# Two feed-forward layers on one core: one more weight pair converted in the first layer, and the second layer's weight requests and input splits at other places

## The chip, the cores and the metric

The program runs on one core of a Trainium2 chip. The time is device microseconds (us) of one execution; lower is better. Three executions of the kernel before are shown, and one more was recorded by the hardware profiler.

## What is computed

An attention with packed keys feeds two dense layers, in float32. Shapes: batch 4, 8 heads, 576 positions, head size 64, 32 packed positions; then x has 2304 rows of 512, and each layer goes 512 to 2048 to 512.

```python
def _attn_ref(q, k, v, p):
    p_packed = sm_attn(p, k, v)
    out = sm_attn(q, p_packed, p_packed)

def _moe_ref(x, w_in, w_out):
    h = x @ w_in
    g = np.maximum(h, 0.0) + np.log1p(np.exp(-np.abs(h)))
    return g @ w_out

def _moe2_ref(x, w_in, w_out):
    h = x @ w_in
    g = h * (1.0 / (1.0 + np.exp(-h)))
    return g @ w_out
```

The weights arrive as 64-bit floating-point numbers; the kernel reads them as pairs of 32-bit words and builds float32 values from them.

## The kernel before

All work is written out in the order in which each engine is to do it: the program's instructions are queued per engine in the order of the code, nothing reorders them, and each engine works its queue front to back. SyncE (SP) issues every transfer, also front to back: a transfer that has to wait for its buffer holds up all transfers behind it.

**Precision.** Every operand of a matrix product is split into a high part (ScalarE rounds it, a copy to the type float32r) and a low part (VectorE subtracts the high part). A product is then three matmuls: low by high, high by low, high by high.

**First layer** (0 to about 370 us). Attention comes first, then 128 short steps (`run_steps`). Each does one 128-wide slice of the hidden layer for 288 rows of x: six matmuls (L482), softplus and split (L494, L495, L499), and twelve matmuls of the output product (L522), added into `ya` (L539). Between them an `agenda` (a list of items by step) places other work: the first layer's own weight conversions (`conv_w`), and conversions for the second layer.

**Conversions for the second layer.** `wi2` comes in 16 slices, two of which make a *pair* `jp` (0 to 7); `wo2` in 16 slices `n`. A conversion of a pair (`conv_pair`, or the fills of `plan_second`) loads two raw slices (`load_raw`, L186), scales them (ScalarE, L135), joins the words (VectorE, L197 and L203), forms four differences (`sums_i`, L218), rounds (`high_i`, L221), subtracts (`low_i`, L225) and stores 1792 KB to a scratch area `wd` in HBM (`store_i`, L232). A slice of `wo2` goes the same way (`high_o` L242, `low_o` L246) and is stored as 512 KB into `od` (`store_o`, L250). In the kernel before, pairs 0 to 2 and slices 0 to 11 are done in the first layer; pairs 3 to 7 and slices 12 to 15 in steps 1 to 5 of the second layer.

**Second layer** (`second`, from about 370 us). 24 steps `k`: three blocks `s` of 768 rows by eight pairs. A step does a 2 by 2 block of the input product with seven products `Q1` to `Q7` in place of eight (a scheme of Strassen's kind, hence the sums and differences), six matmuls of 128 by 384 each (`products`, L833), and four output tiles of twelve matmuls each (`out_tile`, L849), which belong to results of earlier steps. Tile `y0` to `y3` of step k is of group f = (k-2)//2 and needs the split results `G` of steps 2f and 2f+1. Step 1 has no output tiles, step 0 carries the first layer's last ones. In the PE queue of a usual step stand: Q1, Q6, y0, Q2, Q7, y1, Q5, y2, Q3, Q4, y3. ScalarE reads bank A after Q1 (`ta`, L887), and after Q2 applies the silu (`tg`, L901) and splits into `G`; VectorE adds (`add`, L883) `u2`, `u3` and `c2`; Q3 has to wait for the sum `c2` that reads bank C. After Q3 and Q4 come silu and split of `tc` (L926) and `c2` (L938, L939).

**Rings.** The converted weights come back from HBM in chunks of 512 KB: `w<-wd` (`load_i1`, L775; one chunk holds two products' weights) into a ring of five buffers, a chunk requested when the chunk five before it has been used; `w<-od` (`load_o1`, L780) into a ring of eight buffers, two chunks at the end of each step. A chunk of `wd` whose pair isn't stored yet is held back (`held`) until the store is issued; it then waits for the store to land. Group f uses chunks 4f to 4f+3 of `od` in steps 2f+2 and 2f+3.

**Points.** A step calls `go(...)` at fixed places, at which the fills of that point are emitted: L at the start, A0 and D0 after Q6, D1 and A1 ahead of y1, D2 after Q5, S ahead of the last silu, A3 and D3 at the end. The raw and split buffers of the second layer's conversions (the pool `stage`, opened at the end of step 0) lie where the first layer's buffers lay; from step 6 on `xc1`, the split input of block 1, takes their place. `x_sum`, `x_high`, `x_low` (L560, L563, L567) make the split input of the next block, in steps 6 to 8 and 14 to 16.

Of the kernel before, what the change touches and what calls it, by code (L numbers as in the profile page):

```python
# [9 lines left out]
F32R = mybir.dt.float32r  # L10
# [7 lines left out]
P = 128  # L18
B, H, S, D = 4, 8, 576, 64
# [4 lines left out]
NF = DFF // P  # L24
# [3 lines left out]
D1 = D + 1  # L28
# [4 lines left out]
GJ = 4  # L33
# [5 lines left out]
NSUP = T // (2 * N1)  # L39
NJ = NF // 2  # L40
NW = 2 * P
NQ = 7
RI = 5
Q1, Q6, Q2, Q7, Q5, Q3, Q4 = range(NQ)
# [3 lines left out]
def body(ctx, tc, kT, vv, qT, pT, wi1, wo1, wi2, wo2, out):  # L48
# [57 lines left out]
    def plan_load(fn, step):  # L106
        loads.setdefault(step, []).append(fn)
# [3 lines left out]
    wraw, whl, wo_plain = {}, {}, {}  # L111
# [60 lines left out]
    st, raws, o_hl = {}, {}, {}  # L172

    def open_stage(wx_bufs, **kw):
        st["p"] = p = push(stage_stack, "stage", 1, **kw)
        st["wf"] = p.tile([P, NQ + 1, NW], F32, name="wf")
        st["whl"] = p.tile([P, NQ, 2, NW], F32R, name="whl2")
        st["wx"] = wx_bufs

    def close_stage():  # L180
# [37 lines left out]
            nc.vector.tensor_tensor(out=wf[:, o], in0=wf[:, a], in1=wf[:, b], op=ALU.subtract)  # L218

    def high_i(a, b):  # L220
        nc.scalar.activation(out=st["whl"][:, a:b, 0], in_=st["wf"][:, a + 1:b + 1], func=AF.Copy)  # L221

    def low_i(a, b):
# [323 lines left out]
    def xq(s, t, k):  # L547
# [5 lines left out]
    SUMS = {  # L553
        Q5: (X22, X21, X22, ALU.add), Q7: (X21, X11, X21, ALU.subtract),
        Q6: (X11, X22, X11, ALU.subtract), Q3: (X12, X12, X11, ALU.subtract),
    }
# [38 lines left out]
    def plan_all():  # L595
# [15 lines left out]
            plan_load(lambda k=k, n=n: load_w(k, n), load)  # L611
            plan(Item(conv_w(k, n)), (s, s + 1))

        for jp, ss in enumerate(((4, 5, 8, 9, 12), (36, 37, 40, 41, 44), (65, 66, 67, 68, 69))):
            ss = tuple(base(1) + s for s in ss)
            for n in 2 * jp, 2 * jp + 1:
                plan_load(lambda n=n: load_raw("i", n, 3), ss[0] - 4)
            plan(Item(conv_pair(jp)), ss)
            plan_load(lambda jp=jp: store_i(jp), ss[-1])
        for n, s in enumerate((15, 18, 21, 28, 47, 50, 53, 60, 71, 72, 73, 75)):  # L620
            s += base(1)
            plan_load(lambda n=n: load_raw("o", n, 3), s - 3)
            plan(Item(conv_o(n)), (s, s + 1))
            plan_load(lambda n=n: store_o(n), s + 1)
        s = base(3) + XC0
# [139 lines left out]
    fills = {}  # L765
# [11 lines left out]
    def load_o1(m):  # L777
        w = ring_o[m] = wp.tile([P, 2 * DM], F32R, name="w", tag=f"o{m % RING['o']}")
        c = m % NF * 2 * DM
        nc.sync.dma_start(out=w.bitcast(F32), in_=od[:, c:c + 2 * DM])  # L780

    def fill(k, point, fn, *args):
        fills.setdefault((k, point), []).append(lambda: fn(*args))

    def plan_second():
        for jp in range(3, NJ):
            k = jp - 2
            for n in 2 * jp, 2 * jp + 1:
                fill(k - (jp > 3), "L" if jp > 3 else "L0", load_raw, "i", n, 0)
                fill(k, "A0", scale_raw, "i", n, True)  # L790
                fill(k, "D0", plain_i, n, True)
            fill(k, "D1", sums_i)
            fill(k, "A1", high_i, 0, 4)
            fill(k, "A1", high_i, 4, NQ)
            fill(k, "D2", low_i, 0, 4)
            fill(k, "D2", low_i, 4, NQ)
            fill(k, "S", store_i, jp)
        for n in range(12, NF):
            k = n - 11
            fill(k, "L", load_raw, "o", n, 0)  # L800
            fill(k, "A1", scale_raw, "o", n, True)
            fill(k, "D3", plain_o, n, True)
            fill(k + 1, "A0", high_o, n, 1)
            fill(k + 1, "D2", low_o, n)
            fill(k + 1, "S", store_o, n)
        for s in range(1, NSUP):
            for i, q in enumerate((Q1, Q2, Q4, Q5, Q7, Q6, Q3)):
                h, d = divmod(4 * (NJ * s - 2) + i, 4)
                if q in SUMS:
                    fill(h, f"D{d}", x_sum, s, q)  # L810
                fill(h, f"D{d}", x_high, s, q)
                fill(h + (d + 1) // 4, f"D{(d + 1) % 4}", x_low, s, q)

    def second():
        psa_stack.close()
# [50 lines left out]
        def out_of(k, i):  # L866
            if not k:
                (dm, y), = emit_out(NS + i)
                return lambda: finish_out(NS + i, dm, y)
            f, t = divmod(k - 2, 2)  # L870
            if f < 0:
                return lambda: None
            y = out_tile(f, t, i)
            return lambda: add_out(f, t, i, y)

        def step(k):
            nonlocal G
            go = lambda p: [fn() for fn in fills.get((k, p), ())]
# [29 lines left out]
                y.pop(0)()  # L908
            go("D1")
            go("A1")  # L910
            y1 = out_of(k, 1)
            y1()
            products(k, Q5, b["C"], True)
# [28 lines left out]
            go("D3")  # L942
            for i, g in (0, g1), (1, g2):
                frees.setdefault(k // 2 * 2 + 2 + i, []).append(g)
            m = k // 2 * GJ + GJ + k % 2 * 2
            if m + 2 <= NSUP * NF and k > 0 or k == 0:
                for i in range(2):
                    if m + i < NSUP * NF:
                        load_o1(m + i)
            if k == 0:  # L950
                l0_stack.close()
                open_stage(1, side="right", reuse_waits="tile")
            if (k + 1, "L0") in fills:
                for fn in fills[k + 1, "L0"]:
                    fn()

        plan_second()
        for k in range(NSTEP):
# [63 lines left out]
```

## Time and profile before

| | |
|---|---|
| median of 3 runs | 809.77 us (808.24 to 809.95) |
| profiled execution | 810.95 us, of it the span of the profile 809.0 us |
| TensorE busy with matmuls | 764.9 us, 95% of the span |
| VectorE, ScalarE busy | 491.7 us (61%), 363.6 us (45%) |
| mean granted TensorE clock | 0.977 of 2.4 GHz |
| transfers | 145.90 MB, mean 180 GB/s |

The profile shows one execution on the engines PE (TensorE), PEld (its weight loads), DVE (VectorE), ACT (ScalarE) and SP (SyncE, which issues the transfers). Times run from the span's start. A row of the timeline merges equal instructions that follow each other; in brackets stands how long the engine was idle before the row and what released it. Busy shares alone say little here, since the second layer has stretches of different limits; the table by stretch below is cut at the first matmul of each step; its columns are the stretch and its length, the busy time of PE, PEld, DVE, ACT and POOL (instructions in brackets), the granted TensorE clock as a share of 2.4 GHz, the busy share of the transfer engines, and GB/s.

### The profile page before, as it was taken

To read this page: it belongs to the slowest core of one execution; us is meant where nothing else is said; L and a number is where in the kernel's file an instruction comes from. 1 tells how busy PE (TensorE), PEld (TensorE's weight loads), DVE (VectorE), ACT (ScalarE), POOL (GpSimd) and SP (SyncE) were. 2 spreads that over 40 slices of the span, in tenths; PEclk is the share of its full clock that TensorE was granted. 3 is DMA by queue.
4 is the path that set the end of the run, shared out by engine and by line. 5 is a ranking of instruction groups with operands and counts; after the bars stand their busy time and mean duration, and the time that the engine had idled before them with its cause. 6 is when DMAs were issued, how large, how long until landed. Compare 5 with 4: busy or idle time off the path is not lost.

```text
span 809.0 us, 13431 instructions
## 1 busy us (share of the span) xinstructions
PE 764.9 (95%) x5488; PEld 726.6 (90%) x5488; DVE 491.7 (61%) x915; ACT 363.6 (45%) x684; POOL 0.7 (0%) x6
## 2 busy tenths in 40 slices
PE   8999999999999999999598787999999999999998
PEld 7777899999999999999598786999999999999998
DVE  4898877888589878574555663743234564334342
ACT  3687776565456555453342442432323332342230
POOL 0000000000000000000000000000000000000000
PEclk9999999999999999999789699999999999999999
DMA  9944231433543416062885949183562644825602
GB/s 341 344 152 171 84 152 54 163 111 106 183 154 121 156 65 237 27 234 79 286 334 208 375 175 328 75 325 122 204 259 61 252 171 155 318 87 207 239 21 79
DMA packets 38972, 145.90 MB, mean 180 GB/s; under 512 B 4352, under 2 KB 7936, under 8 KB 37376
## 3 DMA queue, kind: packets, MB, share of 16 engines
q1 hardware_dynamic: 38912, 145.06, 48.6%
q8 instruction: 43, 0.70, 0.4%
q14 instruction: 17, 0.14, 0.1%
HBM read 117.25 MB, written 27.79 MB: 179 GB/s over the span
## 4 chain that ended last, share of the span: by engine, by line
PE 75%; DMA 13%; ACT 5%; DVE 4%; SPq 1%; issue 1%; ACTq 0%; DVEq 0%
PE y L522 23%; PE y L849 19%; PE h L482 12%; PE pC L833 6%; DMA w<-wd 6%; PE pA L833 4%; PE pB L833 4%; DMA od<-ohl 3%; PE pD L833 3%; PE psa L448 2%; DMA raw<-wo 2%; PE y L515 2%; DMA wraw<-wo 1%; DMA raw<-wi 1%; PE psa L355 1%
## 5 line engine op out<-in xcount | busy, mean ns | idle before, releaser
L849 PE MATMUL y<-G,w 128*128 128x384 f32 x1152 | 219.5, 340 | 7.0 <-ACT G L927 7.0
L849 PEld LDWEIGHTS y<-G,w 128*128 128x128 f32 x1152 | 206.5, 192 | 7.6 <-ACT G L927 7.3
L522 PE MATMUL y<-gh,w 128*128 128x288 f32 x960 | 213.0, 298 | 0.2 <-DVE ya L537 0.2
L522 PEld LDWEIGHTS y<-gh,w 128*128 128x128 f32 x960 | 160.2, 188 | 13.1 <-issue 4.6
L522 PE MATMUL y<-gl,w 128*128 128x288 f32 x480 | 142.0, 296 | 0.0
L482 PE MATMUL h<-ax,vw 128*128 128x288 f32 x768 | 125.3, 298 | 0.3 <-DVE ax L431 0.3
L482 PEld LDWEIGHTS h<-ax,vw 128*128 128x128 f32 x768 | 109.5, 188 | 2.5 <-DVE ax L431 0.5
L522 PEld LDWEIGHTS y<-gl,w 128*128 128x128 f32 x480 | 90.6, 189 | 0.5 <-DVE gl L499 0.5
L494 ACT ACTIVATE gt<-h 128x288 f32<-128x288 f32 x120 | 48.8, 406 | 86.6 <-PE h L482 81.9
L862 DVE TENSOR_TENSOR ya<-y,ya 128x384 f32<-128x384 f32 x72 | 40.0, 556 | 65.6 <-PE y L849 65.3
L499 DVE TENSOR_TENSOR gl<-gt,gh 128x288 fp32r<-128x288 f32 x120 | 54.3, 453 | 38.7 <-ACT gh L495 38.1
L833 PE MATMUL pA<-xc,w 128*128 128x384 f32 x288 | 61.1, 348 | 14.4 <-DMA w<-wd 11.0
L833 PE MATMUL pC<-xc,w 128*128 128x384 f32 x288 | 59.7, 342 | 12.5 <-DVE c L883 12.5
L833 PEld LDWEIGHTS pA<-xc,w 128*128 128x128 f32 x288 | 51.6, 194 | 18.6 <-issue 13.6
L833 PEld LDWEIGHTS pC<-xc,w 128*128 128x128 f32 x288 | 51.3, 191 | 13.7 <-DVE c L883 13.4
L833 PE MATMUL pB<-xc,w 128*128 128x384 f32 x288 | 61.2, 349 | 1.6 <-DVE tu L883 1.6
L883 DVE TENSOR_TENSOR tu<-ta,pB 128x384 f32<-128x384 f32 x48 | 26.5, 551 | 58.1 <-PE pB L833 55.5
L833 PEld LDWEIGHTS pB<-xc,w 128*128 128x128 f32 x288 | 53.2, 196 | 2.6 <-DVE tu L883 2.6
L495 ACT ACTIVATE gh<-gt 128x288 fp32r<-128x288 f32 x120 | 53.5, 445 | 3.8
L539 DVE TENSOR_TENSOR ya<-y,ya 128x288 f32<-128x288 f32 x104 | 46.9, 453 | 10.7 <-PE y L522 10.5
L926 ACT ACTIVATE tc<-tc 128x384 f32<-128x384 f32 x24 | 12.6, 523 | 90.5 <-DVE tc L883 90.3
L901 ACT ACTIVATE tg<-pA 128x384 f32<-128x384 f32 x24 | 11.6, 485 | 63.3 <-PE pA L833 63.3
(90 smaller groups left out, 791.9 us busy)
## 6 DMA issues: line engine op xcount, KB each, us to landing
w<-wd SPq DMA_DIRECT2D x84, 512.0 KB, 6.8
w<-od SPq DMA_DIRECT2D x48, 512.0 KB, 6.1
wd<-whl SPq DMA_DIRECT2D x8, 1792.0 KB, 9.1
wraw<-wi SPq DMA_DIRECT2D x16, 512.0 KB, 5.8
wraw<-wo SPq DMA_DIRECT2D x16, 512.0 KB, 5.8
raw<-wi SPq DMA_DIRECT2D x16, 512.0 KB, 6.9
raw<-wo SPq DMA_DIRECT2D x16, 512.0 KB, 7.9
od<-ohl SPq DMA_DIRECT2D x16, 512.0 KB, 3.3
```

Source lines behind the costliest of these rows:

```text
L448: nc.tensor.matmul(t[32 * k:32 * k + 32, r, :512 if wide else 256], lhsT=pts[b][rows, k * NP:(k + 1) * NP], rhs=w[rows, :], start=True, st ...
L482: nc.tensor.matmul(h, lhsT=w, rhs=x, start=(i == 0), stop=(i == len(mm) - 1))
L494: nc.scalar.activation(out=gt, in_=h, func=AF.Softplus)
L495: nc.scalar.activation(out=gh, in_=gt, func=AF.Copy)
L499: nc.vector.tensor_tensor(out=gl, in0=gt, in1=gh.bitcast(F32), op=ALU.subtract)
L515: nc.tensor.matmul(y, lhsT=wo_plain[j][:, c], rhs=gs[u - 1, x], start=(j == js[0]), stop=(j == js[-1]))
L522: nc.tensor.matmul(y, lhsT=w[:, c], rhs=g, start=(j == js[0] and m == 0), stop=(j == js[-1] and m == 2))
L539: nc.vector.tensor_tensor(out=acc, in0=y, in1=acc, op=ALU.add)
L833: nc.tensor.matmul(out, lhsT=a, rhs=b, start=start and not i, stop=not start and i == len(mm) - 1, skip_group_check=True,)
L849: nc.tensor.matmul(y, lhsT=a[:, c], rhs=G[:, g, h, j], start=(k % 2 == j == m == 0), stop=(k % 2 == j == 1 and m == 2),)
L862: nc.vector.tensor_tensor(out=acc, in0=y, in1=acc, op=ALU.add)
L883: add = lambda o, i, j, op=ALU.add: nc.vector.tensor_tensor(out=o, in0=i, in1=j, op=op)
```

## The change

It moves one pair (jp = 3) and one slice of `wo2` (n = 12) from the second layer's conversions into the first layer, at new places in its agenda. In the second layer the raw slices of a pair are requested one step ahead at a new point M (between A1 and y1 of that step), the pool `stage` takes its buffer `whl` when `high_i` writes it and not when the pool opens, and `load_o1` asks for chunks of `od` one step later than before: at the end of step k for the chunks 2k+2 and 2k+3 (before: 2k+4 and 2k+5). The splits of x for the next block are spread by a table. No arithmetic is changed.

```diff
@@ -174,7 +174,6 @@
     def open_stage(wx_bufs, **kw):
         st["p"] = p = push(stage_stack, "stage", 1, **kw)
         st["wf"] = p.tile([P, NQ + 1, NW], F32, name="wf")
-        st["whl"] = p.tile([P, NQ, 2, NW], F32R, name="whl2")
         st["wx"] = wx_bufs
@@ -218,6 +217,8 @@
     def high_i(a, b):
+        if not a:
+            st["whl"] = st["p"].tile([P, NQ, 2, NW], F32R, name="whl2")
         nc.scalar.activation(out=st["whl"][:, a:b, 0], in_=st["wf"][:, a + 1:b + 1], func=AF.Copy)
@@ -611,13 +612,15 @@
-        for jp, ss in enumerate(((4, 5, 8, 9, 12), (36, 37, 40, 41, 44), (65, 66, 67, 68, 69))):
+        for jp, ss in enumerate(
+            ((4, 5, 8, 9, 12), (36, 37, 40, 41, 44), (65, 66, 67, 68, 69), (71, 72, 73, 74, 75))
+        ):
...
-        for n, s in enumerate((15, 18, 21, 28, 47, 50, 53, 60, 71, 72, 73, 75)):
+        for n, s in enumerate((15, 18, 21, 28, 47, 50, 53, 60, 24, 33, 56, 76, 77)):
             s += base(1)
@@ -783,10 +786,10 @@
     def plan_second():
-        for jp in range(3, NJ):
+        for jp in range(4, NJ):
             k = jp - 2
             for n in 2 * jp, 2 * jp + 1:
-                fill(k - (jp > 3), "L" if jp > 3 else "L0", load_raw, "i", n, 0)
+                fill(k - 1, "M", load_raw, "i", n, 0)
                 fill(k, "A0", scale_raw, "i", n, True)
...
-        for n in range(12, NF):
+        for n in range(13, NF):
             k = n - 11
...
         for s in range(1, NSUP):
-            for i, q in enumerate((Q1, Q2, Q4, Q5, Q7, Q6, Q3)):
-                h, d = divmod(4 * (NJ * s - 2) + i, 4)
-                if q in SUMS:
-                    fill(h, f"D{d}", x_sum, s, q)
-                fill(h, f"D{d}", x_high, s, q)
-                fill(h + (d + 1) // 4, f"D{(d + 1) % 4}", x_low, s, q)
+            plans = {
+                (0, "D0"): ((x_high, Q1), (x_high, Q2)),
+                (0, "D1"): ((x_high, Q4), (x_low, Q1)),
+                (0, "D2"): ((x_low, Q2), (x_low, Q4)),
+                (0, "D3"): ((x_sum, Q5),),
+                (1, "D0"): ((x_high, Q5), (x_sum, Q7)),
+                (1, "D1"): ((x_low, Q5), (x_sum, Q6), (x_high, Q7), (x_high, Q6)),
+                (1, "D2"): ((x_low, Q7), (x_low, Q6)),
+                (1, "D3"): ((x_sum, Q3),),
+                (2, "D0"): ((x_high, Q3),),
+                (2, "D1"): ((x_low, Q3),),
+            }
...
@@ -908,6 +920,7 @@
             go("D1")
             go("A1")
+            go("M")
             y1 = out_of(k, 1)
@@ -942,17 +955,13 @@
-            m = k // 2 * GJ + GJ + k % 2 * 2
-            if m + 2 <= NSUP * NF and k > 0 or k == 0:
-                for i in range(2):
-                    if m + i < NSUP * NF:
-                        load_o1(m + i)
+            m = (k + 1) // 2 * GJ + (2 - k % 2 * 2)
+            for i in range(2):
+                if GJ <= m + i < NSUP * NF:
+                    load_o1(m + i)
             if k == 0:
                 l0_stack.close()
                 open_stage(1, side="right", reuse_waits="tile")
-            if (k + 1, "L0") in fills:
-                for fn in fills[k + 1, "L0"]:
-                    fn()
```

How the order on the engines moves, at two places. First SP's queue from step 0's end into step 4, in the kernel before (L780 asks for chunks of `od`, L775 for chunks of `wd`, L186 for raw slices, L232 and L250 store):

```order
L780 DMA w<-od 128x1024 x2
L186 DMA raw<-wi 128x512 x4
L186 DMA raw<-wo 128x512
L775 DMA w<-wd 128x1024 x2
L232 DMA wd<-whl_5028 128x3584
L775 DMA w<-wd 128x1024 x2
L780 DMA w<-od 128x1024 x2
L186 DMA raw<-wi 128x512 x2
L186 DMA raw<-wo 128x512
L775 DMA w<-wd 128x1024 x2
L232 DMA wd<-whl_5028 128x3584
L250 DMA od<-ohl 128x1024
```

The same stretch with the change, from the five chunks of `wd` of steps 0 and 1 on (L778 is `load_i1`, L783 `load_o1`, L185 `load_raw`, L233 and L251 the stores):

```order
L778 DMA w<-wd 128x1024 x5
L185 DMA raw<-wi 128x512 x2
L778 DMA w<-wd 128x1024 x2
L783 DMA w<-od 128x1024 x2
L185 DMA raw<-wo 128x512
L778 DMA w<-wd 128x1024 x2
L185 DMA raw<-wi 128x512 x2
L233 DMA wd<-whl_5216 128x3584
L778 DMA w<-wd 128x1024
L783 DMA w<-od 128x1024 x2
L185 DMA raw<-wo 128x512
L778 DMA w<-wd 128x1024 x2
```

The two chunks of `od` at the end of step 0 are gone, step 1 has neither a raw slice of `wo2` nor a store, and the first store of a pair comes one step later.

Second, ScalarE's queue in step 1 and the start of step 2, in the kernel before (from step 1's `ta` to step 2's `tg`):

```order
L887 ACTIVATE ta<-pA 128x384
L135 ACTIVATE raw<-raw 128x512 x2
L901 ACTIVATE tg_5040<-pA 128x384
L902 ACTIVATE G<-tg_5040 128x384
L221 ACTIVATE whl_5028<-wf 128x4x256
L221 ACTIVATE whl_5028<-wf 128x3x256
L135 ACTIVATE raw<-raw 128x512
L926 ACTIVATE tc_5041<-tc_5041 128x384
L927 ACTIVATE G<-tc_5041 128x384
L938 ACTIVATE c_5042<-c_5042 128x768
L939 ACTIVATE G<-c_5042 128x768
L887 ACTIVATE ta<-pA 128x384
```

and with the change:

```order
L899 ACTIVATE ta<-pA 128x384
L913 ACTIVATE tg_5068<-pA 128x384
L914 ACTIVATE G<-tg_5068 128x384
L939 ACTIVATE tc_5069<-tc_5069 128x384
L940 ACTIVATE G<-tc_5069 128x384
L951 ACTIVATE c_5070<-c_5070 128x768
L952 ACTIVATE G<-c_5070 128x768
L899 ACTIVATE ta<-pA 128x384
L135 ACTIVATE raw<-raw 128x512 x2
```

The three scalings of raw slices and the two roundings that stood between step 1's `ta` and its last silu have left step 1.

## Rows read from the trace of the kernel before

**Rows 1.** Busy time by stretch, cut at the starts of steps 1 to 11.
```profile
383.60:399.10 15.50, 8.47 (x44) 8.15 (x43) 8.72 (x16) 5.41 (x9) 0.00 (x0) 0.79 0.72 242
399.10:422.40 23.30, 20.73 (x91) 19.97 (x91) 13.14 (x24) 10.51 (x19) 0.00 (x0) 0.77 0.87 342
422.40:438.00 15.60, 15.60 (x92) 15.60 (x91) 11.71 (x21) 7.52 (x13) 0.00 (x0) 1.00 0.46 174
438.00:465.80 27.80, 20.04 (x93) 18.55 (x92) 13.19 (x24) 9.15 (x16) 0.00 (x0) 0.75 0.97 371
465.80:486.30 20.50, 17.68 (x91) 17.04 (x90) 14.13 (x26) 10.25 (x17) 0.00 (x0) 0.92 0.46 164
486.30:510.00 23.70, 17.75 (x93) 17.14 (x92) 8.36 (x14) 6.84 (x11) 0.00 (x0) 0.93 0.92 341
510.00:526.50 16.50, 16.04 (x92) 15.58 (x92) 13.39 (x20) 6.24 (x10) 0.00 (x0) 1.00 0.04 5
526.50:543.50 17.00, 16.00 (x91) 15.71 (x90) 7.83 (x14) 4.88 (x9) 0.00 (x0) 1.00 0.97 367
543.50:559.30 15.80, 15.80 (x91) 15.80 (x91) 6.89 (x12) 4.21 (x8) 0.00 (x0) 1.00 0.08 20
559.30:576.40 17.10, 16.03 (x92) 15.73 (x91) 5.22 (x9) 4.35 (x9) 0.00 (x0) 1.00 0.99 375
576.40:788.90 212.50, 205.72 (x1173) 203.56 (x1172) 91.55 (x154) 66.69 (x113) 0.00 (x0) 1.00 0.45 169
```

**Rows 2.** Timeline of PE (start, us, what, idle before and releaser): one stall, and a full-clock pair.
```profile
397.06 2.29 PE L833 MATMUL pC<-xc,w 128*128 128x384 f32 x6 [7.03 <-DVE c L883]
...
430.75 1.20 PE L833 MATMUL pC<-xc,w 128*128 128x384 f32 x6
431.79 2.24 PE L849 MATMUL y<-G,w 128*128 128x384 f32 x12
```

**Rows 3.** Timeline of ACT: four waits for transfers.
```profile
401.21 0.67 ACT L135 ACTIVATE raw<-raw 128x512 f32<-128x512 f32 x1 [3.18 <-DMA raw<-wo]
...
446.40 0.65 ACT L135 ACTIVATE raw<-raw 128x512 f32<-128x512 f32 x1 [12.25 <-DMA raw<-wo]
...
475.88 0.63 ACT L242 ACTIVATE ohl<-wx 128x512 fp32r<-128x512 f32 x1 [5.05 <-DMA od<-ohl]
...
499.93 0.85 ACT L563 ACTIVATE xc<-ya 128x768 fp32r<-128x768 f32 x1 [11.87 <-DMA od<-ohl]
```

**Rows 4.** Who SP's queue waited for (engine, line, releaser: us in total, times, longest).
```profile
SPq L780 <- PE y L849: 150.0, 11, 19.2
...
SPq L775 <- DMA wd<-whl: 50.2, 5, 12.0
```

**Rows 5.** Timeline of SP: issues at the end of steps 3 and 5.
```profile
438.78 0.54 SPq L186 DMA_DIRECT2D raw<-wo  x1
...
487.33 0.40 SPq L232 DMA_DIRECT2D wd<-whl  x1
```

**Rows 6.** Timeline of DVE: the last low part of step 5.
```profile
482.36 0.68 DVE L246 TENSOR_TENSOR ohl<-wx,ohl 128x512 fp32r<-128x512 f32 x1
```

**Rows 7.** Who PE waited for, the chunks of `wd`.
```profile
PE pA L833 <- DMA w<-wd: 11.0, 9, 2.5
```

**Rows 8.** Transfers issued between 416 and 432 us (KB each, us to landing).
```profile
od<-ohl SPq DMA_DIRECT2D x1, 512.0 KB, 9.4
```

**Rows 9.** The same between 460 and 476 us.
```profile
od<-ohl SPq DMA_DIRECT2D x1, 512.0 KB, 12.9
```

**Rows 10.** The same between 150 and 170 us, in the first layer.
```profile
wd<-whl SPq DMA_DIRECT2D x1, 1792.0 KB, 7.3
```

**Rows 11.** The page's transfers, chunks of `wd`, median.
```profile
w<-wd SPq DMA_DIRECT2D x84, 512.0 KB, 6.8
```

**Rows 12.** Busy time in a crowded stretch of the first layer.
```profile
160.00:180.00 20.00, 20.00 (x158) 18.77 (x157) 18.01 (x36) 12.58 (x27) 0.00 (x0) 1.00 0.39 147
```

**Rows 13.** Busy time of a stretch in which the transfers are saturated.
```profile
440.00:453.50 13.50, 5.74 (x21) 4.25 (x19) 3.23 (x6) 5.82 (x11) 0.00 (x0) 0.64 1.00 398
```

More of the change, by code (lines that the diff above doesn't have):

```diff
@@ L806, in plan_second @@
         for s in range(1, NSUP):
-            for i, q in enumerate((Q1, Q2, Q4, Q5, Q7, Q6, Q3)):
-                h, d = divmod(4 * (NJ * s - 2) + i, 4)
-                if q in SUMS:
-                    fill(h, f"D{d}", x_sum, s, q)
-                fill(h, f"D{d}", x_high, s, q)
-                fill(h + (d + 1) // 4, f"D{(d + 1) % 4}", x_low, s, q)
+            plans = {
[10 more added lines that the diff above has]
+            }
+            for (h, point), fns in plans.items():
+                for fn, q in fns:
+                    fill(NJ * s - 2 + h, point, fn, s, q)
     def second():
```

## Prediction

> **What bounds the kernel now.** I read the table by stretch first, because the page's shares average over two layers. TensorE sets the pace, but not everywhere. Step 3 of the second layer ran without a gap: 15.6 us, 15.60 of it busy, clock 1.00 [rows 1]. That is the clean step. A product of six matmuls takes 1.04 us (431.79 - 430.75) [rows 2], so an output tile takes (15.6 - 7 x 1.04) / 4 = 2.08 us, and step 1, with seven products and no tile, should take 7.3 us.
>
> Steps 1 to 7 run from 383.6 to 526.5, which is 142.9 us [rows 1]; clean they are 7.3 + 6 x 15.6 = 100.9. So **42.0 us are lost there**. Steps 8 to 23 run from 526.5 to 788.9. There odd steps take 15.8 and even steps 17.0 and 17.1 [rows 1], and PE waited for chunks of `wd` for 11.0 us in nine places [rows 7], one of which (2.5) lies in step 6. With 1.25 us for each of eight even steps, **10.0 us are lost there**. The first layer has no gap to win: PE is busy 20.00 of 20 us even where VectorE is at 18.01 [rows 12].
>
> Why it is lost, read from the waits. SP waited 150.0 us in 11 places at L780, for PE's output tiles [rows 4]: at the end of an even step the kernel asks for two chunks of `od` whose buffers are read until the end of the next step, and for that whole step nothing else leaves SP's queue. Three things come of it. A raw slice of `wo2` left SP at 438.78 [rows 5], after the start of the step that needs it; ScalarE stood 12.25 us until 446.40 [rows 3], and everything behind it on ScalarE, `tc`, `c2` and the next `ta`, stood with it. The last store of a pair left at 487.33 [rows 5] although VectorE had finished its low part by 483.0 (482.36 + 0.68) [rows 6]. And the chunks of `wd` leave late, which is the 1.25 us of the even steps. A second cause is the store itself: `high_o` and the first `x_high` wait until a store has landed, 5.05 us at 475.88 and 11.87 us at 499.93 [rows 3]. Stalls cost more than their length: after 7.03 us without work, six matmuls took 2.29 us in place of about 1.2, and the stretches with stalls had a clock of 0.75 to 0.93 [rows 1, 2], a mix of 2.4 and 1.2 GHz.
>
> **The change, part by part.** The sum is made against the profiled execution, 810.95 us; the median, 809.77, is 1.2 lower, so 1.2 comes off at the end.
>
> *Steps 1 and 2.* Step 1 loses its conversion: two scalings, two roundings and one more scaling stand no longer between its `ta` and its silu, so the wait of 3.18 us at 401.21 [rows 3] and the one behind 397.06 [rows 2] go. Next late is step 2's `ta`. It stands on ScalarE behind step 1's two silus and two copies: three operations of 384 columns and two of 768, and one VectorE sum ahead of them. By columns from 0.67 for 512 and 0.85 for 768 [rows 3] that is 3 x 0.5 + 2 x 0.85 + 0.6 = 3.8 us, of which step 2's Q1 and Q6 cover 2.1. Left: 1.7 (bounds 0 and 3.8). So 15.5 + 23.3 = 38.8 [rows 1] become 7.3 + 15.6 + 1.7 = 24.6: **-14.2**.
>
> *Step 3* stays at 15.6; it now does what step 4 did, and has no store of `od` in front of it.
>
> *Steps 4 to 6*, now 27.8 + 20.5 + 23.7 = 72.0 [rows 1], clean 46.8. The late raw slice goes, since at the end of step 3 SP waits for the last tile only. What stays is a loop: a store lands, `high_o` may run, then `tg`, four differences, `high_i`, `low_i`, `low_o`, and the next store. From `high_o` at 475.88 [rows 3] to the end of `low_o` at 483.04 [rows 6] are 7.2 us; with 0.4 for the issue a loop takes L + 7.6, where L is the landing time. Against 15.6 each step loses L - 8.0. L is not shown for the new order. From below: 7.3 for a pair's store with little beside it [rows 10]. From above: 12.9 [rows 9], where the store had waited in SP's queue until other requests had piled up. Where SP was free when the store was due it took 9.4 [rows 8]. I take 10.5, near 9.4 and somewhat over it, because up to nine requests of 0.52 MB (4.7 MB, 12 us at the 398 GB/s of [rows 13]) are now let go right behind the store before. Three such steps (in step 6 the first `x_high` takes `high_o`'s place: the new `xc1` still waits for the last store as a whole) lose 3 x 2.5 = 7.5. So 72.0 become 54.3: **-17.7**.
>
> *Held chunks.* The last product of steps 4 and 6 needs a chunk that may be read only after the store of the step before has landed: 10.5 + 6.8 [rows 11] = 17.3 us after that store, which leaves about 14.5 us into a step. The product comes 13.6 us later, or 16.1 with the step's loss of 2.5. I take 1.0 each (bounds 0 and 3): **+2.0**.
>
> *Step 7*, 16.5 now [rows 1]: the sums of x stand ahead of `ta` no longer, 15.8: **-0.7**.
>
> *Steps 8 to 23.* Chunks of `od` are asked for when the step's last tile has been issued, and then SP waits for that tile at most, about 2 us. A chunk of `wd` is asked for ten products before its use, over 15.6 us, and lands in 6.8 [rows 11]. The waits go: **-10.0** (bounds -11 and 0). The chunks of `od` come one step later, but still over a step ahead.
>
> *First layer.* It gains one pair and one slice. On VectorE that is, by 0.68 for 512 columns [rows 6], 5888 columns for the pair and 2048 for the slice, 10.5 us, spread over some ten steps. Cost taken: 0. The cover is TensorE's own work; at 18.01 of 20 [rows 12] VectorE is close to full at places, and without any cover it would be +10.5.
>
> Sum: -14.2 - 17.7 + 2.0 - 0.7 - 10.0 = -40.6. 810.95 - 40.6 - 1.2 = **769** us.
>
> **Rivals.**
>
> *Stores land quickly.* SP is free at each store, and L is 8 or less, as the 7.3 of [rows 10]. Then the 7.5 go: 761.5. For it: no request is stuck ahead of the store. Against: 9.4 [rows 8] was already with SP free. The Trainium skill, "DMA: Bandwidth & Descriptors", section "Anatomy of one DMA", puts a transfer at about 2.0 us plus its bytes at 436 GB/s; for the two stores together that is an estimate of 7.4 us, and the sum would be 761.5. By that rule this rival would be the likeliest case; the landings of [rows 8, 9] lie above it. By the rows I leave it a fifth.
>
> *Transfers stay as slow as they are.* Steps 2 to 5 must carry 25.1 MB (per full step 3.5 chunks of `wd`, two of `od`, three raw slices, one pair and one slice stored: 6.8 MB; step 2 has 6.3, step 5 has 5.2). At 398 GB/s that is 63 us, just what the four steps take; but in steps 2 to 5 the kernel before moved only 279 GB/s, the mean of 342, 174, 371 and 164 by length [rows 1]. If that comes of the chain store, wait, reload, and not of SP, the four steps take 90 us where I count 69 (17.3 + 15.6 + 2 x 18.1): 790.
>
> *Even steps keep their wait.* If the 1.25 us come from the ring of five chunks and not from SP, 10 us stay: 779. Against it: odd steps, with the same ring, have none.
>
> *Slower.* The loop of steps 4 to 6 gets longer than what is won. Without any loss in the loop the change is worth 48.1, so it would turn at 3 x (L - 8) = 48.1, L = 24; at 26 it is 816. The longest landing I can point to is 12.9 [rows 9].
>
> *It does not do what it says:* the requests for `od` would still find their buffers in use. By the formula the last reader is the tile just issued, so this is only the 2 us named above.
>
> **How the numbers follow.** The forecast (764 to 775) gets 0.53, quick stores 0.20, slow transfers 0.13, the even steps 0.10, slower 0.03, and 0.01 for no change. About 0.2% (1.6 us) is what a measurement of this kernel can tell from none. Range: from below quick stores with step 2's 1.7 gone as well, 759, to just short of slow transfers, 786. Faster 0.96, same 0.01, slower 0.03.
>
> **What would show it.** SP's wait at L780 for PE falls from 150 to under 30 us; step 1 takes about 7.3 and step 2 about 17 us; no raw slice holds ScalarE for over 3 us; steps 4 to 6 take 17 to 19 us each, with `high_o` waiting for a store; even steps from 8 on equal the odd ones. Wrong would be: a wait for chunks in every even step, landings of 13 us or more in steps 3 to 5, or gaps of PE before 370 us.

## The result, and the profile after

| | before | after |
|---|---|---|
| median of 4 runs | 809.86 us (808.24 to 811.0) | 766.66 us (766.07 to 767.2) |
| profiled execution, span | 810.95, 809.0 us | 766.18, 764.4 us |
| mean granted TensorE clock | 0.977 | 0.997 |

The ratio is 0.9468, with a 95% interval of 0.9449 to 0.9487. The forecast was 769 us.

Busy time by stretch after the change, cut at the starts of steps 1 to 9; the last row runs from 1.5 us before step 16 to 1 us behind step 23 (columns as in [rows 1], to which these rows answer):

```profile
383.30:390.60 7.30, 7.30 (x45) 7.30 (x43) 3.55 (x6) 2.38 (x5) 0.00 (x0) 1.00 0.70 214
390.60:408.20 17.60, 15.94 (x92) 15.53 (x92) 11.65 (x21) 9.91 (x17) 0.00 (x0) 1.00 0.94 374
408.20:423.80 15.60, 15.60 (x92) 15.60 (x91) 11.74 (x21) 9.85 (x17) 0.00 (x0) 1.00 0.92 350
423.80:439.40 15.60, 15.60 (x92) 15.60 (x91) 12.36 (x23) 7.49 (x13) 0.00 (x0) 1.00 0.91 355
439.40:461.40 22.00, 17.60 (x91) 17.05 (x90) 14.13 (x26) 9.91 (x17) 0.00 (x0) 0.92 0.88 335
461.40:477.00 15.60, 15.60 (x92) 15.60 (x91) 9.41 (x15) 6.33 (x11) 0.00 (x0) 1.00 0.86 299
477.00:492.60 15.60, 15.60 (x92) 15.60 (x91) 11.74 (x18) 6.64 (x11) 0.00 (x0) 1.00 0.55 179
492.60:508.40 15.80, 15.80 (x92) 15.80 (x91) 8.54 (x14) 5.08 (x9) 0.00 (x0) 1.00 0.69 229
...
617.70:745.00 127.30, 127.30 (x736) 127.30 (x735) 53.84 (x94) 39.77 (x68) 0.00 (x0) 1.00 0.55 178
```

TensorE is busy without a gap in every row shown but two: step 2 (15.94 of 17.60) and step 5 (17.60 of 22.00, clock 0.92). The timeline of PE has just two rows with a wait between 383 and 480 us:

```profile
394.51 1.32 PE L845 MATMUL pA<-xc,w 128*128 128x384 f32 x6 [1.66 <-ACT ta L899]
...
455.57 1.77 PE L845 MATMUL pC<-xc,w 128*128 128x384 f32 x6 [4.40 <-DVE c L895]
```

Who SP's queue waited for (engine, line, releaser: us in total, times, longest); L783 is now the request for chunks of `od`, 150.0 us in [rows 4]:

```profile
SPq L778 <- DMA wd<-whl: 29.4, 4, 11.9
...
SPq L783 <- PE y L861: 1.3, 7, 0.2
```

ScalarE's two longest waits for transfers in steps 4 and 5, which answer to [rows 3]; the longest is now that of the rounding of a slice for the store before:

```profile
438.83 0.67 ACT L135 ACTIVATE raw<-raw 128x512 f32<-128x512 f32 x1 [3.47 <-DMA raw<-wo]
...
450.97 0.63 ACT L243 ACTIVATE ohl<-wx 128x512 fp32r<-128x512 f32 x1 [4.92 <-DMA od<-ohl]
```

And SP's issues from step 3's stores to step 4's: nine requests leave together once SP has seen the pair's store land, and step 4's stores go behind them.

```profile
420.71 0.33 SPq L233 DMA_DIRECT2D wd<-whl  x1
421.31 0.33 SPq L251 DMA_DIRECT2D od<-ohl  x1
428.66 0.80 SPq L778 DMA_DIRECT2D w<-wd  x2
429.55 0.86 SPq L783 DMA_DIRECT2D w<-od  x2
430.51 0.57 SPq L185 DMA_DIRECT2D raw<-wo  x1
431.17 0.89 SPq L778 DMA_DIRECT2D w<-wd  x2
432.16 0.90 SPq L185 DMA_DIRECT2D raw<-wi  x2
436.82 0.33 SPq L233 DMA_DIRECT2D wd<-whl  x1
437.43 0.33 SPq L251 DMA_DIRECT2D od<-ohl  x1
```

The store of step 3's slice landed 8.5 us after its issue, that of step 4's 13.5. That second landing ends the wait at 450.97.

### The profile page after: what moved, and what is told of

Its sections match the earlier page's. It is cut to its first block, busy times and chain, and to the rows that moved or that the text cites. A ratio compares the mean times of both kernels' runs of the same rounds, so it can differ in the third digit from the quotient of the medians.

```text
span 764.4 us, 13458 instructions
## 1 busy us (share of the span) xinstructions
PE 749.4 (98%) x5488; PEld 716.9 (94%) x5488; DVE 492.4 (64%) x918; ACT 364.3 (48%) x684; POOL 0.7 (0%) x6
## 4 chain that ended last, share of the span: by engine, by line
PE 87%; DVE 4%; ACT 4%; DMA 3%; issue 1%; SPq 1%; ACTq 0%; DVEq 0%
PE y L861 24%; PE y L523 24%; PE h L483 12%; PE pC L845 6%; PE pA L845 6%; PE pB L845 6%; PE pD L845 3%; PE psa L449 2%; DMA od<-ohl 2%; PE y L516 2%; DMA wraw<-wo 1%; PE psa L356 1%; ACT L418 0%; PE psa L404 0%; ACT ax L430 0%
## 5 line engine op out<-in xcount | busy, mean ns | idle before, releaser
L861 PE MATMUL y<-G,w 128*128 128x384 f32 x1152 | 214.7, 335 | 0.0
L861 PEld LDWEIGHTS y<-G,w 128*128 128x128 f32 x1152 | 202.1, 188 | 0.0
L523 PEld LDWEIGHTS y<-gh,w 128*128 128x128 f32 x960 | 160.2, 188 | 12.9 <-issue 3.8
L845 PE MATMUL pA<-xc,w 128*128 128x384 f32 x288 | 58.1, 336 | 1.7 <-ACT ta L899 1.7
L845 PE MATMUL pB<-xc,w 128*128 128x384 f32 x288 | 58.2, 336 | 0.0
L845 PEld LDWEIGHTS pB<-xc,w 128*128 128x128 f32 x288 | 50.8, 188 | 0.3 <-DVE tu L895 0.2
L913 ACT ACTIVATE tg<-pA 128x384 f32<-128x384 f32 x24 | 11.7, 489 | 55.3 <-PE pA L845 55.3
```

Source lines behind the costliest of these rows:

```text
L523: nc.tensor.matmul(y, lhsT=w[:, c], rhs=g, start=(j == js[0] and m == 0), stop=(j == js[-1] and m == 2))
L845: nc.tensor.matmul(out, lhsT=a, rhs=b, start=start and not i, stop=not start and i == len(mm) - 1, skip_group_check=True,)
L861: nc.tensor.matmul(y, lhsT=a[:, c], rhs=G[:, g, h, j], start=(k % 2 == j == m == 0), stop=(k % 2 == j == 1 and m == 2),)
```

## The experiments

Twelve kernels were run, in four groups with one chip each. The kernel before ran beside each group and took 812.41 to 814.44 us in the median, with a wider spread than in the table above, so I compare mainly lengths of steps. They are differences between the first matmuls of consecutive steps on the timeline of PE in the one profiled execution of each kernel, in us:

| step | 1 | 2 | 3 | 4 | 5 | 6 | 7 | 8 |
|---|---|---|---|---|---|---|---|---|
| before | 15.53 | 23.29 | 15.60 | 27.73 | 20.57 | 23.66 | 16.47 | 17.04 |
| after | 7.31 | 17.58 | 15.60 | 15.60 | 22.05 | 15.60 | 15.60 | 15.82 |
| A: after, old requests for od | 7.30 | 17.60 | 15.60 | 26.40 | 22.84 | 23.97 | 15.60 | 16.96 |
| B: before, new requests for od | 9.64 | 22.54 | 17.89 | 19.56 | 20.53 | 15.60 | 16.49 | 15.82 |
| C: old splits, old whl | 7.30 | 17.58 | 15.60 | 15.60 | 20.99 | 15.60 | 16.46 | 15.82 |
| D: raw slices at L | 7.31 | 17.57 | 15.60 | 16.29 | 22.23 | 15.60 | 15.60 | 15.82 |
| E: slice's store first | 7.32 | 17.59 | 15.60 | 15.60 | 16.76 | 22.98 | 15.60 | 15.82 |
| F: xc1 at a multiple of 64 | 7.29 | 17.58 | 15.60 | 15.76 | 21.94 | 15.59 | 15.61 | 15.68 |
| G: y0 early, xc1 at 128 | 7.30 | 15.60 | 15.60 | 18.13 | 23.20 | 15.60 | 15.60 | 15.60 |
| H: slices in the first layer | 7.30 | 17.58 | 15.60 | 15.60 | 15.60 | 15.74 | 15.60 | 15.82 |
| I: H and six idle transfers | 7.29 | 17.59 | 15.60 | 15.60 | 15.60 | 21.80 | 15.60 | 15.82 |
| K: G and H | 7.32 | 15.60 | 15.60 | 15.60 | 15.60 | 18.13 | 15.60 | 15.60 |
| L: K, splits later | 7.30 | 15.60 | 15.60 | 15.60 | 15.60 | 15.60 | 15.60 | 15.60 |

The theory behind the prediction: SP stood for whole steps at requests for `od` whose buffers were in use, and that cost steps 4 to 6 and every even step; moving the pair gave step 1. The main rival: the smaller volume of transfers relieved steps 4 to 6, and the ring of five made the even steps wait.

### A. The requests for od, undone

```diff
-            m = (k + 1) // 2 * GJ + (2 - k % 2 * 2)
-            for i in range(2):
-                if GJ <= m + i < NSUP * NF:
-                    load_o1(m + i)
+            m = k // 2 * GJ + GJ + k % 2 * 2
+            if m + 2 <= NSUP * NF and k > 0 or k == 0:
+                for i in range(2):
+                    if m + i < NSUP * NF:
+                        load_o1(m + i)
```

> The changed kernel with the old requests for chunks of od: asked for one step earlier, so at the end of every even step the two buffers are still being read for a whole further step. Theory (SP's queue stands behind these requests, and that made the loss both in steps 4 to 6 and in every even step from 8 on): the even steps take 17.0 again in place of 15.6 to 15.8, which is 8 x 1.25 = +10 us, and steps 4 to 6 go from 53.3 back towards 72, +15 to +19; together 791 to 796 us, with a wait of SP for the output tiles of about 150 us. Rival (steps 4 to 6 were relieved because one pair and one slice less are carried through them): only the even steps come back, 777 us. Rival (the even steps' wait came from the ring of five chunks, and the volume did the rest): 767 us.

Measured: 801.89 us, 0.984 of the kernel before beside it (0.9793 to 0.9887). Steps 4 to 6 take 73.2 us, as before the change (72.0), although the pair and the slice are out of them. From the start of step 8 to that of step 23 it took 249.8 us, against 235.8 after the change and 246.8 before it. SP waits at the requests for `od` as long as it did before the change (150.0 us in [rows 4]):

```profile
SPq L783 <- PE y L861: 153.9, 15, 17.1
```

SP's timeline from step 3 to the start of step 4 (424.45) in this kernel:

```profile
411.35 0.33 SPq L778 DMA_DIRECT2D w<-wd  x1
423.08 1.04 SPq L783 DMA_DIRECT2D w<-od  x2
424.23 0.36 SPq L185 DMA_DIRECT2D raw<-wo  x1
```

For 11.7 us nothing leaves the queue, then the raw slice for step 4 comes too late, and ScalarE waits 10.19 us for it:

```profile
430.15 0.65 ACT L135 ACTIVATE raw<-raw 128x512 f32<-128x512 f32 x1 [10.19 <-DMA raw<-wo]
```

The stretch of step 3 shows the empty transfer engines, and that of step 4 the price:

```profile
408.85:424.45 15.60, 15.60 (x91) 15.60 (x91) 11.18 (x20) 7.41 (x12) 0.00 (x0) 1.00 0.24 84
424.45:450.85 26.40, 20.19 (x91) 18.38 (x91) 13.01 (x24) 9.26 (x16) 0.00 (x0) 0.81 0.94 355
```

In step 3 this kernel moved 84 GB/s where the changed kernel moved 350. The theory holds; less volume alone did not relieve steps 4 to 6. The total lies above the 791 to 796 I expected: against the changed kernel the even steps from 8 on cost 14.1 us in place of 10, and steps 4 to 6 cost 20.0 in place of 15 to 19.

### B. The requests for od, alone

The kernel before, with the diff of A turned round as its only change.

> The kernel before with the new requests for chunks of od as the only change; the pair and the slice stay in the second layer. Theory: steps 1 and 2 keep their 38.8 us, the even steps from 8 on lose 10 us, steps 4 to 6 lose 14 to 18 us: 782 to 786 us. Rival (volume): steps 4 to 6 stay at 72 us or within 3 of it, and only the even steps gain: 797 to 800 us.

Measured: 779.8 us, 0.9566 (0.9515 to 0.9617) of the kernel before. Steps 4 to 6 fall from 72.0 to 55.7, and steps 8 to 22 lose their waits (10.4 us in all), as the theory says. It is better than expected because steps 1 and 2 fall as well, from 38.8 to 32.2: there too the raw slices stood behind two requests for `od`, at the end of step 0. Step 3 rises by 2.3. A is the other half of the comparison (the whole change but the requests): steps 1 and 2 take 24.9 there, as after the change. So in steps 1 and 2 the requests alone give 6.6 of the 13.9 us won, and the move gives all of it with the old requests in place. Over steps 1 to 7: before 142.9, B 122.3, A 129.3, after 109.3. The requests give 20.6 alone and 20.0 on top of the move, the move 13.5 alone and 12.9 on top of the requests: the two add up over the stretch, though not step by step. Alone the requests win in steps 1, 2 and 4 to 6, on top of the move in steps 4 to 6 only.

### C and D. The smaller parts, undone

C puts the splits of x back to the old loop and takes `whl` when `stage` opens; D asks for the raw slices at L.

```diff
-                fill(k - 1, "M", load_raw, "i", n, 0)
+                fill(k - 1, "L", load_raw, "i", n, 0)
```

> The changed kernel with two of the change's smaller parts undone: the splits of x for the next block at their old places, and the buffer whl taken when the pool stage opens. They act at different steps. Theory: the old places cost 0.9 us in step 7 and 0.7 in step 15, as the kernel before had them there (16.47 and 16.5 in place of 15.60 and 15.82); the buffer costs nothing, since xc1 waits for the last store as a whole either way, so steps 2 to 6 stay at 17.6, 15.6, 15.6, 22.0 and 15.6. Together +1.6 us, 768.3. Rival: the buffer taken at once holds up the first pair of the second layer, steps 2 to 6 grow by 2 us or more: 770 or over.

> The changed kernel with the raw slices of a pair requested where they were before, at the start of the step ahead and not at point M behind A1. Theory (the place matters little once the requests for od are out of the way, because SP stands behind a store until 4 to 5 us into steps 3 to 5 anyway, and by then the raw buffers are free): 0 to +2 us, 766.7 to 768.7, at most a longer wait of ScalarE for the raw slice of wo2, which now stands behind the two. Rival (point M was as much of the gain as the requests for od, because a raw slice asked for before its buffer is free stops SP just as well): steps 3 to 6 lose 2 us or more each, 773 or over.

Measured: C 766.87 us (0.9403 to 0.9476 of the kernel before), D 765.91 (0.9389 to 0.9447); the changed kernel, run again beside I, had 0.9401 to 0.9452. C shows the splits' 0.86 in step 7 and 0.7 in step 15, and its steps 2 to 4 and 6 are the same to 0.01: the place of `whl` costs nothing. Its step 5 is 1.06 shorter, which I don't count, since the unaltered kernel had 22.05 in one profile and 21.34 in another. In D ScalarE waits longer for the raw slices of `wo2` (7.15 us in step 5 at most), but the steps change by under 1 us. Point M is no part of the gain that can be measured.

### E. What is left in step 5

The stall of step 5 came from the rounding of a slice that waited for the slice's last store. E issues that small store ahead of the pair's.

```diff
-            fill(k, "S", store_i, jp)
...
             fill(k + 1, "S", store_o, n)
+        for jp in range(4, NJ):
+            fill(jp - 2, "S", store_i, jp)
```

> The changed kernel with the slice's store issued ahead of the pair's store in each of steps 3 to 5. Theory (what is left is one stall in step 5, in which the rounding of the slice stands first in ScalarE's queue and waits 4.9 us for the 512 KB store of step 4, which went out behind nine requests and the pair's 1792 KB): the small store lands several us earlier, the wait goes, and with it the stall of 4.4 us and the time at the lower clock, 6.4 us in step 5 at most: 760 to 763 us. Rival (the wait only passes to the next in ScalarE's queue, the rounding of the pair, which needs the pair's store to have landed): 765 to 767 us, no difference.

Measured: 768.72 us (766.52 to 770.04), no gain. The wait went, and step 5 fell to 16.76; but step 6 rose to 22.98. ScalarE's timeline in E:

```profile
452.17 1.80 ACT L222 ACTIVATE whl<-wf 128x1024 fp32r<-128x1024 f32 x2 [2.64 <-DMA wd<-whl]
...
468.97 1.58 ACT L564 ACTIVATE xc<-ya 128x768 fp32r<-128x768 f32 x2 [8.96 <-DMA wd<-whl]
```

The pair's store of step 5 was issued at 456.44, close behind five other requests (452.14 to 454.6), and took 12.4 us; the first split into `xc1` waited for it. My theory for this run was wrong: the stall was moved, not removed.

### G and F. A wait of TensorE, and an address

G brings y0 of step 2 ahead of Q2, to cover the wait for `ta`; G and F also move `xc1` (G by 96 bytes per partition, F by 32).

```diff
-            late = k in (1, 2)
+            late = k == 1
...
-        xcs[n] = pool(f"xc{n}", 1, **kw).tile([P, NQ, 2, 2, N1], F32R, name=f"xc{n}")
+        xp = pool(f"xc{n}", 1, **kw)
+        xcs[n] = xp.tile([P, NQ, 2, 2, N1], F32R, name=f"xc{n}")
+        if n:
+            xp.tile([P, 24], F32, name="pad")
```

> The changed kernel with two additions that act at different steps: in step 2 the tile y0 stands ahead of Q2 again, as in step 3 and later, and xc1 begins at 186240, a multiple of 128 as the address of xc0 is (with a multiple of 64 steps 8 to 15 took 15.68 in place of 15.82). Theory: y0 covers the 1.7 us in which TensorE waits in step 2 for ta, so step 2 takes 15.9 to 16.4 in place of 17.6 (-1.2 to -1.7); steps 8 to 15 take 15.60 like all others (-1.8 in all). Rivals: y0 itself has to wait for G of step 1 and step 2 stays at 17.6; steps 8 to 15 stay at 15.68 or 15.82 whatever the address is, because the rest comes of other work beside them.

> The changed kernel with 32 bytes per partition added to the pool of xc1, so that xc1 begins 32 bytes lower, at 186304, a multiple of 64 as the address of xc0 is (139392). Steps 8 to 15, which read xc1, take 15.82 us each, the steps that read xc0 15.60. Theory (the matmuls read xc1 a little more slowly because of where it lies): 8 x 0.22 = -1.8 us, steps 8 to 15 at 15.60: 764.9. Rival (the difference comes from other work beside these steps): no change, 766.7.

Measured: G 765.3 us, F 764.95. In G step 2 takes 15.60, all 2.0 us are won; steps 4 and 5 then lose 3.7 more than they did, and step 7 begins 95.4 us after step 1, against 93.7 in the changed kernel. As in E something gained ahead was given back. Steps 8 to 15 took 15.60 in G: the address is the whole difference there (shown in the last section).

### H and I. Is it the volume?

Steps 2 to 5 run at 335 to 374 GB/s, with the 25.1 MB to carry that the prediction worked out. H takes 3.1 MB out: the slices 13 to 15 are converted in the first layer. I puts the same bytes back as six transfers of raw slices that nothing computes with.

```diff
-        for n, s in enumerate((15, 18, 21, 28, 47, 50, 53, 60, 24, 33, 56, 76, 77)):
+        for n, s in enumerate((15, 18, 21, 28, 47, 50, 53, 60, 24, 33, 56, 76, 77, 30, 44, 62)):
...
-        for n in range(13, NF):
+        for n in range(16, NF):
```

```diff
+    def load_more(n):
+        t = st["p"].tile([P, DM], I64, name="more", bufs=2)
+        nc.sync.dma_start(out=t, in_=wsrc["o"][1][n])
...
+        for n in range(13, NF):
+            fill(n - 11, "L", load_more, n)
+            fill(n - 10, "S", load_more, n)
```

> The changed kernel with the last three slices of wo2 converted in the first layer too, in steps where VectorE is least busy. Theory (what is left in steps 3 to 6 is the loop of store, landing and next rounding in a stretch whose transfers run near 350 to 370 GB/s; 3.1 MB less in steps 2 to 5 is 8 us of transfer): the stall of step 5 goes, step 5 takes 15.6 to 16.5 and step 6 stays at 15.6, first layer +0 to +1: 760 to 762. Rival (the loss only passes on to step 6, where the first split into xc1 waits for the last store of a pair, as when the slice's store went first): 765 to 767. Rival (VectorE is full in the first layer): step 0 begins 2 us or more later and eats up part of it.

> The kernel with all slices of wo2 converted in the first layer, and six more transfers of 512 KB in steps 2 to 5 that nothing reads and nothing waits for: one at the start of steps 2, 3 and 4, where the raw slice stood, and one behind the pair's store of steps 3, 4 and 5, where the slice's store stood. So the volume of the changed kernel is back, without its scalings, roundings and waits. Theory (volume set the 6.4 us): the loss comes back in steps 4 to 6, 4 to 7 us, 764 to 767. Rival (the single buffer of the slices, with its wait of ScalarE for the store before, set it): 760 to 761.

> The changed kernel once more, unaltered, on the same chip as the next two, as their measure: 765 to 768 us, step 2 at 17.6, step 5 at 21 to 22.3 us.

Measured: H 760.02 us (759.53 to 760.34), I 766.61 (765.78 to 767.41), the changed kernel beside I 766.52. Steps 5 and 6 in H, then in I:

```profile
440.09:455.69 15.60, 15.60 (x92) 15.60 (x91) 12.12 (x22) 7.23 (x12) 0.00 (x0) 1.00 0.83 310
455.69:471.43 15.74, 15.74 (x92) 15.58 (x91) 9.11 (x15) 5.77 (x10) 0.00 (x0) 1.00 0.80 314
```

```profile
440.24:455.84 15.60, 15.60 (x92) 15.60 (x91) 12.06 (x22) 6.92 (x12) 0.00 (x0) 1.00 0.88 321
455.84:477.64 21.80, 17.35 (x92) 17.03 (x91) 9.31 (x15) 6.73 (x11) 0.00 (x0) 0.92 0.89 330
```

With the bytes back, and none of the work or the roundings' waits, the loss is back too: 6.2 us, in step 6. The expectation was wrong in one point: something did wait for the idle transfers. `xc1` lies where their buffers lay, and its first split waited until 466.94 for the last of them:

```profile
466.94 1.58 ACT L568 ACTIVATE xc<-ya 128x768 fp32r<-128x768 f32 x2 [9.37 <-DMA more<-wo]
```

The pair's store, issued at 452.91, had landed after 12.7 us, at 465.6. So the split came 11.1 us into step 6, where in H it came 6.5 us into it; 1.3 of these 4.6 us come from that wait, and 3.3 from the store's own late landing (9.9 us after its issue in H). How the 6.2 us divide between the two isn't shown. What H and I show is that bytes without work bring back a loss, and most of the delay comes by way of the store. That the rate of the transfers alone sets it isn't shown: the transfer engines were busy for 0.80 to 0.89 of these two steps. Whatever I moved, step 7 began 92.7 to 95.9 us after step 1 wherever the bytes were all there (the changed kernel, C to G, I), and 87.4 after it in H. The first layer took the three slices without a visible cost: step 1 starts at 384.01 in H and between 383.00 and 385.13 in all runs.

### K and L. G and H joined, then the splits later

> The changed kernel with all slices of wo2 converted in the first layer, y0 of step 2 ahead of Q2, and xc1 at a multiple of 128. Theory (with the volume gone from steps 2 to 5 the 2.0 us won in step 2 are not given back in steps 4 and 5, as they were without that; steps 8 to 15 gain 0.22 each): 760.0 - 2.0 - 1.8 = 756.3 us, every step from 2 on at 15.6. Rival (the gain of step 2 is given back again whatever the volume): 758.3 us.

K joins G and H: 759.18 us (756.62 to 760.73). Again the 2.0 us of step 2 came back, now as 2.5 in step 6: the rival was right, the gain was given back with 3.1 MB less to carry too. I took it that what stands behind the wait is what matters, so L moves the first splits one point later (`x_high` of Q1 and Q2 from D0 to D1, and what follows them by one point).

```diff
-                (0, "D0"): ((x_high, Q1), (x_high, Q2)),
-                (0, "D1"): ((x_high, Q4), (x_low, Q1)),
-                (0, "D2"): ((x_low, Q2), (x_low, Q4)),
-                (0, "D3"): ((x_sum, Q5),),
+                (0, "D1"): ((x_high, Q1), (x_high, Q2)),
+                (0, "D2"): ((x_high, Q4), (x_low, Q1)),
+                (0, "D3"): ((x_low, Q2), (x_low, Q4), (x_sum, Q5)),
```

> The last kernel with the first splits into xc1 one point later in step 6: behind the silu and split of tg, not ahead of them. In the last kernel the end of the pair's last store (12.4 us behind its issue) came 8.9 us into step 6, and with ScalarE everything that Q3 needs stood until then: 2.5 us. Theory (the transfers end when they end; what counts is who stands behind the wait): with only the silu of tc behind it, which comes 5 us after that, step 6 takes 15.6 and the 2.0 us won in step 2 are kept: 756.2 us on a chip like that of the run before last, 2 to 3 us under the last kernel. Rival (the splits, 2 to 3 us later now, are late themselves for Q1, Q2 and Q4 of step 8 or stand in the way of c2): step 6 or 7 keeps 2 us or more, 758 to 760.

ScalarE in step 6 of K, then of L:

```profile
462.24 1.58 ACT L567 ACTIVATE xc<-ya 128x768 fp32r<-128x768 f32 x2 [7.17 <-DMA wd<-whl]
463.72 0.47 ACT L916 ACTIVATE tg<-pA 128x384 f32<-128x384 f32 x1
```

```profile
458.49 0.49 ACT L915 ACTIVATE tg<-pA 128x384 f32<-128x384 f32 x1 [3.67 <-PE pA L847]
459.02 0.53 ACT L916 ACTIVATE G<-tg 128x384 fp32r<-128x384 f32 x1
460.91 2.32 ACT L567 ACTIVATE xc<-ya 128x768 fp32r<-128x768 f32 x3 [1.36 <-DMA wd<-whl]
```

L takes 756.14 us (755.65 to 757.24), 0.9295 of the kernel before (0.9262 to 0.9328). Every step from 2 on is at 15.60 and the clock is 1.00. The store still lands 11.2 us after its issue (K 12.3), and the wait for it ends 7.8 us into step 6 (K 8.9), but `tg` no longer stands behind the wait, and the silu of `tc` comes over 5 us after it. L is faster than the changed kernel: its interval meets neither that of the result (0.9449 to 0.9487) nor that of the changed kernel run again (0.9401 to 0.9452). That it is faster than K or H isn't shown: its interval overlaps both of theirs (K 0.9304 to 0.936, H 0.9322 to 0.9368). L's order without H, at the full volume, was not tried.

## Why the prediction was right

*What bounds the kernel.* The clean step of 15.6 us and the 42.0 and 10.0 us lost against it were the right measure: in L all of it is gone, steps 1 to 7 taking the 100.9 us that were worked out. The cause named first, SP's wait at the requests for `od`, is shown by A and B.

*Steps 1 and 2:* -14.2 predicted, -13.9 measured (7.31 + 17.58 against 38.82). The wait of 1.7 us for step 2's `ta`, worked out from the row lengths, was 1.66. The reason given, the conversion that leaves step 1, is enough for the whole of it: A has 24.90 with the old requests. B shows that the requests for `od`, which the prediction did not count here, take off 6.6 where they stand alone; on top of the move they give nothing in these two steps.

*Step 3:* 0 and 0.

*Steps 4 to 6:* -17.7 predicted; from 71.96 to 53.25 is -18.7. The sum was close and the spread was not: I counted L - 8.0 = 2.5 in each step, and step 5 alone lost 6.45. The landings were 8.5, 13.5 and 8.3 us for the slices' stores of steps 3, 4 and 5, around the 10.5 I took, and the formula with each landing gives 5.5 for step 5, and 0.5 and 0.3 for the other two. So the loop was priced right and the landing time was not one number; that the sum came out within 1 us is partly luck, since two steps below the 2.5 made up for one above it. The landing goes with what was still in flight. Of the nine requests ahead of step 4's stores six had not landed when the slice's store left, and the last landed at 445.35; of the eight ahead of step 3's it was three, of the five ahead of step 5's one. The bound from above, 12.9 of [rows 9], was passed by 0.6, and it was not the longest landing of the kernel before either: there a slice's store issued at 440.95 took 13.7. By the Trainium skill, "DMA: Bandwidth & Descriptors", section "Anatomy of one DMA", I had estimated 7.4 us for the two stores. That section gives its figure for transfers that GpSimd issues, and SP issues these; the traces show 8.3 to 13.5, and the measurement decides.

*Held chunks:* +2.0 predicted, nothing measured. No product in steps 1 to 23 waited for a chunk of `wd`. The chunks were asked for when the store had landed, at 428.66 and 429.07 for step 4, and landed 3.6 and 4.5 us later, where the sum took the 6.8 of [rows 11]; so they were there by 433.55, and step 4's last product came at 436.26. In step 5 the stall itself gave the time.

*Step 7:* -0.7 and -0.9; C shows that this is the table of the splits.

*Steps 8 to 23:* -10.0 predicted, 246.8 to 235.8 measured, -11.0. Odd and even steps are equal. By A and B it is the requests, not the ring of five; B, which has the old splits, wins 10.4, and C shows the other 0.7 in step 15.

*First layer:* 0 predicted; step 1 starts at 383.29 (before 383.61). In H even three more slices cost nothing there.

*The sum.* The profiled execution became 44.8 us shorter, where the sum had 40.6. The 2.0 for the held chunks, and 1.0 each in steps 4 to 6 and from step 8 on, are nearly all of that.

*The signs.* SP's wait at the requests for `od` fell to 1.3 us, and steps 1 and 2 took the lengths named. Three signs came out against the forecast: steps 4 to 6 took 15.6, 22.05 and 15.6 us where 17 to 19 each were expected, a raw slice held ScalarE for 3.47 us at 438.83 where 3 was the most, and one store took 13.5 us, where 13 or more was named as a sign of being wrong. The first and the third are the landing of a store, the second that of a raw slice, 8.3 us after its issue.

*The rivals.* "Even steps keep their wait" and "slower" did not happen. "Stores land quickly" fell with the 13.5 of step 4, though steps 4 and 6, with landings of 8.5 and 8.3, lost nothing. "Transfers stay as slow as they are" was wrong as a forecast (790), but its volume matters for the rest: steps 2 to 5 took 70.8 us at about 352 GB/s (the mean of the four stretches by length), where the sum counted 69. H shows that taking three conversions, 3.1 of the 25.1 MB worked out for that rival, out of these steps takes the loss that was left away; I shows that putting as many bytes back without the work brings a loss back. E and G fit that but don't prove it, since K gave its 2.0 us back at the smaller volume, and in L, at that volume, another order alone left no loss.

## What to carry to other kernels

A request whose buffer is not free yet stops its whole queue: ask for the data when the last reader has been issued, and look for the price in transfers that have nothing to do with that buffer. Where a stretch has several waits for crowded transfers, an edit to one wait can move the stall to the next, as in E, G and K; compare the start of the step behind the whole stretch, not the length of one step. What helped here was fewer bytes there (H), and then a wait with nothing urgent behind it (L).

## What the runs showed of the hardware

Steps 8 to 15 take 15.82 us and all other clean steps 15.60, at the same clock of 1.00, before and after the change. They differ in the buffer that their products read: `xc0` begins at byte 139392 of each partition, a multiple of 128, `xc1` at 186336, which is 32 above a multiple of 64. Two products of step 9 on the timeline of PE, in the changed kernel:

```profile
508.45 1.22 PE L845 MATMUL pA<-xc,w 128*128 128x384 f32 x6
509.50 1.22 PE L845 MATMUL pB<-xc,w 128*128 128x384 f32 x6
510.56 0.34 PE L861 MATMUL y<-G,w 128*128 128x384 f32 x1
```

The same in G, with `xc1` at 186240, a multiple of 128:

```profile
509.68 1.20 PE L848 MATMUL pA<-xc,w 128*128 128x384 f32 x6
510.72 1.20 PE L848 MATMUL pB<-xc,w 128*128 128x384 f32 x6
511.76 0.33 PE L864 MATMUL y<-G,w 128*128 128x384 f32 x1
```

A product takes 1.05 to 1.06 us there and 1.04 here, and the step 15.82 and 15.60, 1.8 us over eight steps. The products are not all of it: of the 0.22 us of step 9 they have 0.13, and 0.09 lies in three of the four output tiles, which take 2.11 in place of 2.08 although they read other buffers. At 186304 (F), a multiple of 64 but not of 128, steps 8 to 15 took 15.68: products at 1.04, but all four output tiles still at 2.11. Why the output tiles change with this address was not tried.
